# A fused H3 and MLP kernel on one core: all four convolution blocks through the factored transform, in smaller matmul tiles

## The chip, the cores and the metric

The kernel runs on one core of a Trainium2 chip. Its time is the device time of one execution in microseconds (us). Two runs of the kernel before took 268.71 and 269.87 us, a median of 269.29 us. The profile below is of one more execution.

## The reference

Two layers, each an H3 mixer (A) and a channel MLP (B), run over a sequence of 2048 tokens with 512 channels. Both layers use the same weights, and k and v are inputs, so the long convolution of `kv` is the same in both layers and is computed once.

```python
def _A_ref(q, k, v, shift_k, ssm_k, ssm_D):          # S = 2048, D = 512
    k_shift = sum over t of k_pad[:, t:t + S, :] * shift_k[:, ks - 1 - t]   # 4 taps
    kv = k_shift * v
    y = irfft(rfft(kv padded to 2S) * rfft(ssm_k padded to 2S))[:S]         # causal, per channel
    y = y + kv * ssm_D
    return q * y
def _B_ref(x, w1, b1, w2, b2):                       # F = 1376
    h = gelu(layernorm(x) @ w1 + b1)
    return h @ w2 + b2
x = A_q
x = x + _A_ref(layernorm(x), A_k, A_v, A_shift_k, A_ssm_k, A_ssm_D)
x = x + _B_ref(layernorm(x), B_w1, B_b1, B_w2, B_b2)
# and both once more
```

## The kernel before, in words

**Blocks.** The sequence is cut into four blocks of 512 tokens, numbered 0 to 3. The causal convolution is done block by block in a frequency domain of 512 odd frequencies: K0 to K3 are the transforms of the four pieces of the filter, U0 to U3 those of the four blocks of kv, and output block j is the inverse transform of the sum of U(a) times K(j-a) for a from 0 to j. Everything is bf16 in one large SBUF arena, with each buffer's place given in the table PLACE.

**Pieces and their order.** The program is a list of named pieces. The string ORDER gives the order in which they are issued and, behind the point, the engine: P (TensorE, PE), D (VectorE, DVE), A (ScalarE, ACT), G (GpSimd, POOL), S (the SP queue, for DMAs). Each engine works through its pieces strictly in that order. A digit behind P is the PSUM slot: four slots, p0 to p3, of two banks each. The names are, with the block first among the digits:

- lK, lk, lv, lx, w1, w2: loads of filter, k, v, q and the weights; lT, lF, lW, lM, lY: loads of the transform tables
- KT, kt: PE transposes of the filter and of k (L373, L394); kv: the 4-tap shift as matmuls with diagonal matrices (L414), and kvm: the product with v on DVE (L425)
- KD, UD: a direct transform of a block (L451), 8 matmuls of 128x128x512 for each quarter of the frequencies
- KS, US: first stage of the factored transform (L476), 128x128 tiles; Kx, Ux: two DMAs each that regroup its result from partition to partition (`regroup`, L294); KW, UW: second stage (L485) in 64x64 tiles
- ks: swaps of real and imaginary halves of K between partitions, by DMA (L436)
- T: products U times K on DVE (L507); V: first inverse stage (L520), 64x64 tiles; Vx: its regroup by DMA; Y: second inverse stage (L533)
- a letter e behind a PE piece's name is its evacuation from PSUM, 128x1024 each, on ACT (L248) or DVE (L250)
- sa, pa, aa, ga, sb, pb, ab: LayerNorms and the gate x + q*y of layer l and block g (the index is 2g+l); dw and dr: the normed activations go out to DRAM and come back transposed; m1, ge, m2, re: the MLP (L621 in six pieces of up to two 128-column groups, GELU on ACT L628, L641, residual L649); st: output stores

**Which block goes which way.** `DK = {0, 1}` and `DU = {0, 1}` send blocks 0 and 1 of K and U through the direct transform (L446 to L467), with 1 MB of tables tabT. Blocks 2 and 3 go through the factored one. The filter's partner K1 adds K0's swapped halves on DVE (L457).

**What sets the order around the change.** The first MLP matmul, piece m101 on L621, needs the convolution of block 0, its gate and two LayerNorms. Before it PE has the transforms; behind it PE alternates between MLP pieces and the transforms that are left.

## Time and profile before

| | us |
|---|---|
| median of two runs | 269.29 (268.71 and 269.87) |
| profiled execution, span from first to last instruction | 269.2 |
| PE busy in it | 246.4 |
| ACT busy, DVE busy | 144.9, 178.0 |
| first matmul starts | 4.59 |
| first MLP matmul (m101) starts | 87.35 |
| last matmul ends | 262.66 |

The profiled execution's own time is its span, 269.2 us, which lies between the two timed runs. PE's busy time counts a matmul until its result is out, so pipelined matmuls overlap, and a busy PE is not PE at its peak. A time such as "379 ns mean" is the latency of one matmul, and the pace of a run of them is its length divided by their number. PEclk is the granted TensorE clock. "Idle before" a group is time in which that engine stood still, with what ended it.

### The profile page before, as it was taken

What the parts mean: (1) busy time and instruction counts of PE and PEld (TensorE: products, weight loads), DVE (VectorE), ACT (ScalarE), POOL (GpSimd) and SP (SyncE); (2) the same over time, 40 slices, a digit from 0 to 9 for tenths busy, and PEclk for the clock granted to TensorE, in tenths of its full rate; (3) what the DMA queues carried; (4) which work ended last, traced back from release to release, by engine and by line L of the source; (5) the groups of instructions that cost most, each with busy time, mean ns of one, the idle gap of its engine ahead of it and who ended that gap; (6) DMA issues with size and microseconds to landing.
All of it is one profiled execution on the core that took longest, in us unless ns stands there. A gap on an engine that the chain in (4) does not pass through costs nothing.

```text
span 269.2 us, 4359 instructions
## 1 busy us (share of the span) xinstructions
PE 246.4 (92%) x1664; PEld 116.2 (43%) x1664; DVE 178.0 (66%) x293; ACT 144.9 (54%) x187; POOL 45.6 (17%) x89
## 2 busy tenths in 40 slices
PE   3699975999939999999999999999999999999990
PEld 3354533544324444544444444444444444444440
DVE  1558792599846997997999996598770088405021
ACT  2248915579826776698676577600489008303600
POOL 3125300001500003212062015320311011200000
PEclk9999997799977999999999999999999999999997
DMA  6996993496666791767566004135502300330045
GB/s 195 316 220 171 236 289 77 121 243 162 201 177 160 203 305 54 171 147 212 138 162 150 0 2 116 44 100 133 121 0 78 78 2 0 117 78 2 0 108 127
DMA packets 37927, 35.11 MB, mean 130 GB/s; under 512 B 17777, under 2 KB 33650, under 8 KB 37650
## 3 DMA queue, kind: packets, MB, share of 16 engines
q1 hardware_dynamic: 37442, 33.68, 47.7%
q0 software_dynamic: 464, 1.15, 1.5%
q8 instruction: 13, 0.21, 0.4%
q14 instruction: 8, 0.07, 0.1%
HBM read 12.80 MB, written 5.77 MB: 69 GB/s over the span
## 4 chain that ended last, share of the span: by engine, by line
PE 80%; DMA 8%; ACT 4%; DVE 2%; issue 1%; SPq 1%; POOL 1%; ACTq 0%; DVEq 0%; POOLq 0%
PE p L641 28%; PE p L621 28%; PE p L520 7%; PE p L451 6%; PE p L476 3%; ACT arena L248 3%; DMA arena<-tabT 3%; PE p L414 3%; DMA arena<-arena 3%; DMA arena<-in_B_w_dram 3%; PE p L533 2%; PE p L485 1%; SPq L316 1%; ACT arena L287 1%; DVE arena L425 1%
## 5 line engine op out<-in xcount | busy, mean ns | idle before, releaser
L248 ACT ACTIVATE arena<-p 128x1024 bf16<-128x1024 f32 (+2 forms) x66 | 67.8, 1075 | 43.5 <-PE p L451 10.3
L628 ACT ACTIVATE arena<-p,B 128x512 bf16<-128x512 f32 (+1 forms) x88 | 54.7, 687 | 57.1 <-PE p L621 56.3
L621 PE MATMUL p<-arena 128*128 128x512 bf16 (+1 forms) x352 | 78.0, 379 | 0.0
L641 PE MATMUL p<-arena 128*128 128x512 bf16 (+1 forms) x352 | 77.6, 379 | 0.0
L621 PEld LDWEIGHTS <-arena 128*128 128x128 bf16 (+1 forms) x352 | 34.8, 100 | 41.4 <-issue 1.7
L641 PEld LDWEIGHTS <-arena 128*128 128x128 bf16 (+1 forms) x352 | 33.9, 98 | 42.0 <-issue 1.5
L277 POOL TENSOR_TENSOR lrs<-lrs,mhalf 128x2 f32<-128x2 f32 (+1 forms) x29 | 25.7, 888 | 152.0 <-DVE lrs L271 94.7
L507 DVE TENSOR_TENSOR arena<-arena 128x2048 bf16<-128x2048 bf16 (+1 forms) x36 | 46.6, 1336 | 3.1 <-ACT arena L248 1.3
L649 DVE TENSOR_TENSOR arena<-p,arena 128x1024 bf16<-128x1024 f32 (+1 forms) x18 | 19.5, 1102 | 43.2 <-PE p L641 34.8
L267 DVE BATCH_NORM_STATS2 lst<-arena 128x6 f32<-128x512 bf16 x64 | 40.7, 682 | 0.3
L451 PE MATMUL p<-arena 128*128 128x512 bf16 x128 | 32.0, 406 | 2.6 <-DMA arena<-tabT 2.3
L287 ACT ACTIVATE arena<-arena,lnm,lrs 128x512 bf16<-128x512 bf16 x30 | 22.6, 811 | 7.9 <-POOL lnm L282 7.7
L520 PE MATMUL p<-arena,Mt 64*64 64x512 bf16 x320 | 22.2, 416 | 0.0
L451 PEld LDWEIGHTS <-arena 128*128 128x128 bf16 x128 | 12.9, 104 | 19.7 <-issue 5.1
L425 DVE TENSOR_TENSOR arena<-p,arena 128x1024 bf16<-128x1024 f32 x8 | 9.7, 1222 | 10.3 <-PE p L414 7.3
L289 DVE TENSOR_SCALAR arena<-arena,lmv,lrs 128x512 bf16<-128x512 bf16 x34 | 13.1, 433 | 4.7 <-POOL lrs L277 2.6
L520 PEld LDWEIGHTS <-Mt 64*64 64x64 bf16 x320 | 9.0, 114 | 9.6 <-issue 3.5
L593 DVE TENSOR_TENSOR arena<-arena 128x2048 bf16<-128x2048 bf16 (+1 forms) x9 | 9.9, 1105 | 4.0 <-ACT arena L248 3.7
L373 PE MATMUL p<-IDt,arena 128*128 128x128 bf16 x64 | 5.1, 242 | 8.2 <-DMA arena<-in_A_ssm_k_dram 4.6
L250 DVE COPY arena<-p 128x1024 bf16<-128x1024 bf16 (+1 forms) x6 | 5.2, 866 | 11.0 <-PE p L373 5.7
L476 PE MATMUL p<-arena,Ft 128*128 128x512 bf16 x48 | 12.0, 380 | 0.0
L250 DVE CAST arena<-p 128x1024 bf16<-128x1024 f32 x8 | 9.8, 1220 | 3.1 <-PE p L451 1.6
(44 smaller groups left out, 108.3 us busy)
## 6 DMA issues: line engine op xcount, KB each, us to landing
arena<-arena SPq DMA_DIRECT2D x80, 128.0 KB, 2.4
lnd<-arena SPq DMA_DIRECT2D x14, 256.0 KB, 2.2
arena<-in_A_ssm_k_dram SPq DMA_DIRECT2D x4, 512.0 KB, 8.5
arena<-in_A_k_dram SPq DMA_DIRECT2D x4, 512.0 KB, 4.5
arena<-arena SPq DMA_DIRECT2D x8, 256.0 KB, 3.7
arena<-in_A_v_dram SPq DMA_DIRECT2D x3, 512.0 KB, 8.6
arena<-in_A_q_dram SPq DMA_DIRECT2D x6, 256.0 KB, 8.8
out_dram<-arena SPq DMA_DIRECT2D x12, 128.0 KB, 2.4
```

What stands on the lines that cost most here:

```text
L248: nc.scalar.activation(dst, src, AF.Copy)
L267: nc.vector.bn_stats(lst[:, i, :], xg[:, i, :])
L277: nc.gpsimd.tensor_tensor(self.rs[:, a:b], self.rs[:, a:b], mhalf[:, a:b], ALU.pow)
L287: nc.scalar.activation(dst[:, i, :], xg[:, i, :], AF.Identity, bias=self.nm[:, i:i + 1], scale=self.rs[:, i:i + 1])
L451: nc.tensor.matmul(o[:, r, :], at(f"TD{i}", (n * 2 + r) * P, [[1, P]]), at(src, n * D, [[1, D]]), start=n == 0, stop=n == 3)
L476: nc.tensor.matmul(o[:, R, :], Ft[:, f, R, :], at(t, n * D, [[1, D]]), start=s == 0, stop=s == len(terms) - 1, skip_group_check=True)
L507: e.tensor_tensor(at(t, 0, [[2 * D * w, 2], [1, 2 * D * w]]), at(f"U{a}", 2 * i * D, [[0, 2], [1, 2 * D * w]]), at(f"K{kk}", 2 * i * D, [[ ...
L520: nc.tensor.matmul(o[64 * r:64 * r + 64, e, :], Mt[64 * e:64 * e + 64, 2 * i + r, s, :], at(f"T{j}{a}{i // TW[j]}", (s * 2 * TW[j] + 2 * ( ...
L621: nc.tensor.matmul(o[0:m, x, :], at("W1", ct * F + ft * P, [[1, m]]), at(LT, ct * 4 * P, [[1, 4 * P]]), start=ct == 0, stop=ct == CT - 1)
L628: nc.scalar.activation(at(HT, ft * 4 * P, [[1, 4 * P]], 0, m), o[0:m, x, :], AF.Gelu_apprx_tanh, bias=B1[0:m, ft:ft + 1])
L641: nc.tensor.matmul(o[:, x, :], at(HT, ft * 4 * P + t * P, [[1, P]], 0, m), at("W2", ft * D, [[1, D]], 0, m), start=ft == 0 and i not in RE ...
L649: nc.vector.tensor_tensor(xs, psum(pe, [2, D])[:, 0:len(tt), :], xs, ALU.add)
```

## The change

The direct transform, its tables tabT, the swaps by DMA (`ks`) and the sum on K1 (`both`) are gone. All four blocks of K and U go through the factored transform, and real and imaginary part lie side by side in the free dimension. The tiles change: the first stage has two 64x128 tiles (rows by columns of the array) at a time in place of one 128x128, the second stage eight 64x32 tiles in place of four 64x64, and V eight 32x64 tiles in place of four 64x64. V now covers half of a block's frequencies in one piece, with four banks of PSUM and two evacuations (Ve, Vf). PSUM is one tile of eight banks, and the digit behind P is now the first bank. The filter's transposes come as two halves of 64 columns, k's shifted copies need one more copy on DVE (kd), k and v are loaded with two DMAs each instead of one. ORDER and PLACE are new throughout. The MLP's arithmetic is the same.

```diff
-DK = {0, 1}
-DU = {0, 1}
...
-    F = np.zeros((128, 2, 2, 128))
-    W = np.zeros((128, 8, 64))
-    M = np.zeros((128, 8, 2, 64))
-    T = np.zeros((4, 128, 4, 2, 128))
+    F = np.zeros((128, 2, 128))
+    W = np.zeros((128, 8, 2, 32))
+    M = np.zeros((128, 2, 2, 3, 64))
...
-        pf = [ps.tile([P, 1024], F32, name=f"p{i}") for i in range(NPS)]
+        pall = ps.tile([P, 8, 512], F32, name="pall")
...
-                            nc.tensor.transpose(o[:, n, cc, :], at(f"Kraw{j}", cc * L + c * nn + n, [[4, P]]), IDt[:])
+                            for R in range(2):
+                                nc.tensor.transpose(o[64 * R:64 * R + 64, n, cc, :], at(f"Kraw{j}", cc * L + 4 * R + c * nn + n, [[8, 64]]), IDt[:])
...
+            def twice(it, j=j):
+                e = nc.vector if it["eng"] == "D" else nc.gpsimd
+                e.tensor_copy(at(f"kT{j}", 1, [[KI, CT * 4], [1, 63]]), at(f"kT{j}", 128, [[KI, CT * 4], [1, 63]]))
...
-        def swaps(j):
...
-                        for p in range(2):
-                            queue(it["eng"]).dma_start(at(f"K{j}", 8 * D + c * w, [[1, w]], 64 * e + 32 * p, 32), at(f"K{j}", c * w, [[1, w]], 64 * e + 32 - 32 * p, 32))
...
-                if j in (DK if X == "K" else DU):
-                    for i in range(4):
-                        def mms(o, i=i, src=src):
-                            for r in range(2):
-                                for n in range(4):
-                                    nc.tensor.matmul(o[:, r, :], at(f"TD{i}", (n * 2 + r) * P, [[1, P]]), at(src, n * D, [[1, D]]), start=n == 0, stop=n == 3)
...
                 for n in range(4):
                     def mms(o, n=n, terms=terms):
                         for s, (t, f) in enumerate(terms):
                             for R in range(2):
-                                nc.tensor.matmul(o[:, R, :], Ft[:, f, R, :], at(t, n * D, [[1, D]]), start=s == 0, stop=s == len(terms) - 1,
-                                                 skip_group_check=True)
+                                nc.tensor.matmul(o[:, R, :], Ft[64 * R:64 * R + 64, f, :], at(t, n * D, [[1, D]], 64 * R, 64), start=s == 0, stop=s == len(terms) - 1)
...
-                        for e in range(2):
-                            for r in range(2):
-                                nc.tensor.matmul(o[64 * e:64 * e + 64, r, :], Wt[64 * r:64 * r + 64, 2 * i + e, :],
-                                                 at(f"zi{X}{j}", (2 * i + e) * D, [[1, D]], 64 * r, 64), start=True, stop=True, skip_group_check=True)
+                            for q in range(4):
+                                for kk in range(2):
+                                    nc.tensor.matmul(o[32 * q:32 * q + 32, kk, :], Wt[64 * kk:64 * kk + 64, 4 * g + q, p, :],
+                                                     at(f"zi{X}{j}", (4 * g + q) * D, [[1, D]], 64 * kk, 64), start=True, stop=True)
...
-                                    nc.tensor.matmul(o[64 * r:64 * r + 64, e, :], Mt[64 * e:64 * e + 64, 2 * i + r, s, :],
-                                                     at(f"T{j}{a}{i // TW[j]}", (s * 2 * TW[j] + 2 * (i % TW[j]) + r) * D, [[1, D]], 64 * e, 64),
-                                                     start=2 * a + s == 0, stop=2 * a + s == n - 1, skip_group_check=True)
+                        for t in range(4):
+                            for kk in range(2):
+                                for q in range(4):
+                                    nc.tensor.matmul(o[64 * kk:64 * kk + 64, q, :], Mt[32 * q:32 * q + 32, g, kk, (0, 2, 2, 1)[t], :],
+                                                     at(f"T{j}{a}{g}", (2 * t + kk) * D, [[1, D]], 32 * q, 32), start=a == 0 and t == 0, stop=a == j and t == 3)
...
 ORDER = """
...
-ge74.A m170.P0 ge72.A m173.P3 ge70.A m175.P2 ge73.A ge75.A m271.P1 m272.P0 re71.D st71.S st32.S m273.P3 re72.D st72.S
...
+US03e.A Ux03.S US00e.A sa20.D pa20.G Ux00.S Kx02.S KT10.P0 ke1.G Kx00.S sa02.D sa00.D lv2.G aa20.D KT10e.A KS11.P0
...
+ge55.A m154.P6 ge54.A ge50.A m153.P6 ge53.A m252.P6 m250.P2 re60.D st30.S st32.S st10.S sa70.D re62.D sa72.D pa70.G
...
+ge71.A m172.P0 ge72.A m170.P4 ge70.A m174.P0 ge74.A m175.P4 ge75.A m272.P4 re72.D st72.S m270.P5 m273.P4 m271.P0 re52.D
...
```

**Place 1, PE, the first transposes of a further filter block.** Before, this is KT20 (L373), which reads the loaded filter and writes slot p3; the last matmul above it is of a direct transform, KD11 (L451). DMAHW names are the SP queue's DMA semaphores, of which there are eight that the queue's DMAs take in turn.

```order
L451 MATMUL p_135<-arena 128x512
L373 LDWEIGHTS arena [waits DMAHW7_49,DMAHW6_49,DMAHW4_49]
L373 MATMUL p_138<-IDt,arena 128x128 [waits Activation_49]
L373 LDWEIGHTS arena
L373 MATMUL p_138<-IDt,arena 128x128
```

After, it is KT10 (L333), behind the first stage of U0 (US02, US03, US01, US00 on L402).

```order
L402 LDWEIGHTS Ft
L402 MATMUL pall<-arena,Ft 128x512
L333 LDWEIGHTS arena [waits DMAHW4_49,DMAHW5_49,DMAHW3_49,DMAHW6_49,DMAHW2_49,DMAHW7_49,DMAHW1_49,DMAHW0_49]
L333 MATMUL pall<-IDt,arena 64x128 [waits Activation_49]
L333 LDWEIGHTS arena
```

The transposes now wait for DMAs on all eight semaphores instead of three, and the matmuls right above them are the four pieces whose results these DMAs carry.

**Place 2, SP queue, the DMAs around the first blocks.** Before, behind the load of K1's piece of the filter, the swaps of K0 (L436) stand between table and block loads.

```order
L316 DMA arena<-in_A_ssm_k_dram 128x4x512 [waits DMAHW6_49]
L436 DMA arena<-arena 32x2048 [waits DMAHW7_49,Activation_49]
L436 DMA arena<-arena 32x2048 [waits DMAHW0_49]
L316 DMA Mt<-tabM 128x1024 [waits DMAHW1_49]
L436 DMA arena<-arena 32x2048 [waits DMAHW2_49]
L436 DMA arena<-arena 32x2048 [waits DMAHW3_49]
L316 DMA Yt<-tabY 128x64 [waits DMAHW4_49]
```

After, behind the same load, come the regroups of K0 and U0, two DMAs to a piece: Kx03, Kx01, the table lW, then Ux02, Ux01, Ux03, Ux00 and Kx02.

```order
L276 DMA arena<-in_A_ssm_k_dram 128x4x512 [waits DMAHW2_49]
L276 DMA arena<-arena 16x8x512 [waits DMAHW3_49,Activation_49]
L276 DMA arena<-arena 16x8x512 [waits DMAHW4_49]
L276 DMA arena<-arena 16x8x512 [waits DMAHW5_49,Activation_49]
L276 DMA arena<-arena 16x8x512 [waits DMAHW6_49]
L276 DMA Wt<-tabW 128x512 [waits DMAHW7_49]
L276 DMA arena<-arena 16x8x512 [waits DMAHW0_49,Activation_49]
L276 DMA arena<-arena 16x8x512 [waits DMAHW1_49]
L276 DMA arena<-arena 16x8x512 [waits DMAHW2_49,DVE_49]
```

The swaps are gone, and ten regroup DMAs stand in one row between US02's evacuation and KT10.

**Place 3, PE, the end of the last MLP block.** Before, the last m1 piece (m175, the last 96 hidden columns, L621) writes slot p2 (printed p_137), and the m2 piece behind it (m271, L641) writes slot p1 (p_136).

```order
L621 LDWEIGHTS arena
L621 MATMUL p_137<-arena 96x512
L641 LDWEIGHTS arena [waits Activation_49]
L641 MATMUL p_136<-arena 128x512
L641 LDWEIGHTS arena [waits Activation_49]
```

After, m175 (L543) and m272 (L561) both stand on bank 4 in ORDER.

```order
L543 LDWEIGHTS arena
L543 MATMUL pall<-arena 96x512
L561 LDWEIGHTS arena
L561 MATMUL pall<-arena 128x512 [waits Activation_49]
L561 LDWEIGHTS arena
```

The first m2 matmul, which writes PSUM, now has a wait for ACT of its own: the GELU that reads the bank of the piece just ahead of it.

462 lines of the change are left out of this document (195 added, 267 removed).

## The prediction

> **What bounds the kernel now.** I read the page's busy line and chain first, then a table of four stretches cut at the first matmul (4.59), at the first MLP matmul m101 (87.35) and at the last result of PE (262.66).
>
> ```profile
> PE 246.4 (92%) x1664; PEld 116.2 (43%) x1664; DVE 178.0 (66%) x293; ACT 144.9 (54%) x187; POOL 45.6 (17%) x89
> PE 80%; DMA 8%; ACT 4%; DVE 2%; issue 1%; SPq 1%; POOL 1%; ACTq 0%; DVEq 0%; POOLq 0%
> ```
> ```profile
> core 0: us, PE busy (x) PEld busy (x) DVE busy (x) ACT busy (x) POOL busy (x), PEclk, DMA share, GB/s
> 0.00:4.59 4.59, 0.00 (x0) 0.00 (x0) 0.00 (x0) 1.28 (x1) 2.55 (x11) 1.00 0.57 193
> 4.59:87.35 82.76, 71.14 (x612) 36.73 (x613) 57.39 (x84) 48.96 (x50) 14.07 (x28) 0.92 0.75 198
> 87.35:262.66 175.31, 175.30 (x1056) 79.46 (x1052) 119.96 (x209) 94.67 (x137) 28.93 (x50) 1.00 0.37 97
> 262.66:269.20 6.54, 0.00 (x0) 0.00 (x0) 0.69 (x1) 0.00 (x0) 0.00 (x0) 0.71 0.52 122
> ```
>
> From 87.35 on PE stands still for 0.01 us: there, less PE work is less time, and each new wait of PE is lost time. Ahead of it PE is idle for 82.76 − 71.14 = 11.6 us, while ACT and DVE are busy for 49 and 57 of the 83 us. So the time is 4.59 to the first matmul + 246.4 busy + 11.7 idle + 6.54 tail = 269.2. The span stands between the two timed runs, so I forecast against 269.2.
>
> **PE's work.** The groups that the change replaces, and two runs for the pace:
>
> ```profile
> L451 PE MATMUL p<-arena 128*128 128x512 bf16 x128 | 32.0, 406 | 2.6 <-DMA arena<-tabT 2.3 <-ACT arena L248 0.4
> L476 PE MATMUL p<-arena,Ft 128*128 128x512 bf16 x48 | 12.0, 380 | 0.0
> L485 PE MATMUL p<-arena,Wt 64*64 64x512 bf16 x64 | 6.2, 412 | 4.9 <-DMA arena<-arena 4.9
> L520 PE MATMUL p<-arena,Mt 64*64 64x512 bf16 x320 | 22.2, 416 | 0.0
> L520 PEld LDWEIGHTS <-Mt 64*64 64x64 bf16 x320 | 9.0, 114 | 9.6 <-issue 3.5 <-DVE arena L507 0.4
> ```
> ```profile
> 90.46 3.56 PE p L621 x16
> 158.47 7.03 PE p L520 x128
> ```
>
> A full-array matmul takes 3.56/16 = 0.22 us. The 64x64 tiles take 7.03/128 = 0.055, so four run side by side in one pass of 0.22. Their 320 weight loads of 0.114 us would fill 36.5 us end to end, but PEld is busy for 9.0: they overlap by four too. Removed: 32.0 + 12.0 + 6.2 + 22.2 = 72.4 us, which is 128 + 48 + 16 + 80 = 272 passes (59.8) and 12.6 for changes of tile shape and slower stretches over 64 pieces, 0.2 a piece. Added: the first stage has 88 matmuls (8 for K0, 16 for each other K, 8 for each U) in pairs, 44 passes; the second 256 in eights, 32 passes; V 640 in eights, 80 passes. That is 156 passes or 34.3 us, and 72 pieces at 0.2 are 14.2. PE: 246.4 − 72.4 + 48.5 = 222.5, so 24 us less, **if eight small tiles run side by side**, which no row here shows. If only four do, V takes 35.1 instead of 17.6 and the second stage 14.1 instead of 7.0.
>
> The Trainium skill, "TensorE: Matmul & The Clock Gate", section LDWEIGHTS, gives a weight load as columns/1.2 ns, estimated 53 ns for V's 64 columns. One after another, eight would be 0.43 us and V 34 us, as with four tiles. The PEld row above has loads of 64 columns overlapping by four, so it doesn't hold as a serial cost here, and the sum goes without it.
>
> **PE's waits.** PE has less to do, but what feeds it stays: evacuations, regroups, and their order. First from PE's timeline and from the chain of waits (start, length, what):
>
> ```profile
> 4.59 1.89 PE L373 MATMUL p<-IDt,arena 128*128 128x128 bf16 x16 [4.59 <-DMA arena<-in_A_ssm_k_dram]
> 6.28 1.91 PE L394 MATMUL p<-IDt,arena 128*128 128x128 bf16 x16
> 10.45 6.47 PE L451 MATMUL p<-arena 128*128 128x512 bf16 x16 [2.25 <-DMA arena<-tabT]
> 16.85 1.95 PE L414 MATMUL p<-arena 64*128 64x256 bf16 x56
> 42.56 1.06 PE L373 MATMUL p<-IDt,arena 128*128 128x128 bf16 x16 [3.60 <-DMA arena<-arena]
> ```
> ```profile
> 19.15 1.21 DVE arena L425
> 33.30 0.56 PE p L520 x8
> 47.14 1.82 PE p L414 x27
> 57.54 0.99 PE p L414 x28
> ```
>
> Then the regroups' time to landing (DMA issues of the page), ten of their issues on SP's timeline, and the groups of ACT, DVE and PE by shape:
>
> ```profile
> arena<-arena SPq DMA_DIRECT2D x80, 128.0 KB, 2.4
> ```
> ```profile
> 61.10 6.42 SPq L316 DMA_DIRECT2D arena<-arena  x10
> ```
> ```profile
> L248 ACT ACTIVATE arena<-p 128x1024 bf16<-128x1024 f32 x60 | 58.7, 1024 | 33.8 <-PE p L451 10.3 <-PE p L520 9.9 <-PE p L485 7.2
> L248 ACT ACTIVATE arena<-p 128x2048 bf16<-128x2048 bf16 x4 | 7.4, 1873 | 5.2 <-DMA arena<-arena 5.2
> L628 ACT ACTIVATE arena<-p,B 128x512 bf16<-128x512 f32 x80 | 49.9, 687 | 40.2 <-PE p L621 39.4 <-DMA arena<-arena 0.8
> L287 ACT ACTIVATE arena<-arena,lnm,lrs 128x512 bf16<-128x512 bf16 x30 | 22.6, 811 | 7.9 <-POOL lnm L282 7.7
> L556 ACT ACT_TABLE_LOAD x1 | 1.3, 1283 | 0.0
> L250 DVE CAST arena<-p 128x1024 bf16<-128x1024 f32 x8 | 9.8, 1220 | 3.1 <-PE p L451 1.6 <-PE p L533 1.4 <-PE p L476 0.2
> L250 DVE COPY arena<-p 128x1024 bf16<-128x1024 bf16 x4 | 2.8, 689 | 7.2 <-PE p L373 5.7 <-ACT arena L248 1.4
> L457 DVE SCALAR_TENSOR_TENSOR arena<-arena,sgn,p 128x1024 bf16<-128x1024 bf16 x4 | 5.1, 1278 | 1.4 <-PE p L451 1.4
> L373 PE MATMUL p<-IDt,arena 128*128 128x128 bf16 x64 | 5.1, 242 | 8.2 <-DMA arena<-in_A_ssm_k_dram 4.6 <-DMA arena<-arena 3.6
> L641 PE MATMUL p<-arena 128*128 128x512 bf16 x320 | 74.3, 379 | 0.0
> ```
>
> A change of tile shape costs 0.12: eight L520 are two passes, 0.44, and took 0.56. (The 0.2 a piece above holds slower stretches too.)
>
> I walk down the new order and take each place where PE has nothing to run.
>
> (a) Up to US02. The 2.25 us for tabT goes. But U0 can't start before v is loaded and both kvm are done; before, these end at 19.15 + 1.21 = 20.4, and with the table wait gone I take 17.5. PE has some 8.5 us to do in the 12.9 us since 4.59 (KT0 1.9, kt0 1.9, kt10 1.9, both kv 1.95, KS0 0.9): **4.5 idle** (2.3 to 6).
>
> (b) KT10 (place 1). It waits on all eight DMA semaphores, that is for Ux01, Ux03, Ux00 and Kx02. Before, such transposes, KT20, waited 3.60 us for regroups, with direct transforms ahead to fill the time. Now: US02 and its evacuation 1.4, ten DMAs issued at 0.64 each (nine to the last: 5.8), landing 2.4: 9.6 us from US02, of which US02 to US00 fill 0.9. **8.7 idle** (3.6 to 9). Behind KT10 on PE stands everything else.
>
> (c) KS11 needs KT10's evacuation, 128x2048 on ACT, 1.87, and the hand-overs: **2.2 idle**.
>
> (d) KS11 to US12: ACT has 20 evacuations in a row, 1.024 and a gap each, 21 us; DVE has some 19 beside it: eight products, kvm twice and four evacuations at 1.22, kd1 and a LayerNorm. PE's work is 8.8 us of passes and kv (four KS1 1.76, three US1 0.66, twelve second-stage pieces 2.64, V0 1.76, kv10 and kv11 1.98) and 2.3 of tile changes, so **10 idle** (6 to 12). Before, a direct piece of 1.76 us on PE stood against each evacuation of 1.02.
>
> The Trainium skill, "TensorEngine Tiling (Array Packing)", section PSUM Bottleneck, speaks against this change: it says that tiling speeds up TensorE but not the evacuation, so that the PSUM copy may become the bottleneck. The rows agree in kind: a second-stage piece is 0.22 us on PE against 1.02 on ACT.
>
> (e) KT20 again stands behind regroups: V0's eight and Ux10, Ux11, Ux13, six, 9.0 us of issue, some 2.5 of it covered: **6.5 idle** (3.6 as KT20 before, to 9).
>
> (f) From there to m101: ACT has kt20's 1.87, 15 evacuations (15.8), two LayerNorm rows (1.6) and the GELU table (1.3), 20.6 us, and Y1 waits for V1's regroup, 2; PE's work is 13.6 (KS2 1.76, UW1 0.88, Y0 and Y10 1.3, V1 3.5, kv2 2.0, KT20 and LT 1.9, US20 0.2, and 17 changes of shape 2.0): **9 idle** (5 to 11).
>
> (g) Place 3. Seven times PE writes the bank whose GELU has just become possible: m145 to m242, m135 to m232, m165 to m260, m155 to m154 to m153 to m252, m175 to m272. Each costs the result's latency (0.16: 379 ns less the pace of 220), the GELU 0.687 and two semaphores, about 0.95: **6.7** (4 to 7.5). Nothing else is left to hide it, since PE takes its pieces in order.
>
> Idle in sum: 4.5 + 8.7 + 2.2 + 10 + 6.5 + 9 + 6.7 = 47.6, where 11.7 stood.
>
> Edits at nothing: the swaps' 24 issues leave SP, but 32 regroups join it, priced in (b) and (e). The four K1 sums on DVE (1.28 each) go and four copies kd come, which no row shows: 0.69 as the L250 copy of that size or 1.22 as the cast, taken at 0.7; DVE has that to spare in (d). KT's transposes in halves are twice as many and, in pairs, take the 5.1 us of L373; if halves don't pair, 5 more, most of it in the front's gaps. k and v cost four more issues each; w1, w2 and lv move to POOL, where a root of a LayerNorm waits at most one or two issues. The tail of 6.54 (residual, store) stays.
>
> **Sum:** 4.6 + 222.5 + 47.6 + 6.5 = 281.2, so **281 us**, 4.4% slower. m101 would start near 85 us: hardly earlier than the 87.35 now, with more of blocks 2 and 3 still to do behind it.
>
> **Rivals.** The time is 233.6 + the idle, so break-even is 35.6 us of idle.
>
> *PE stays the bound (faster).* The waits in (b), (d), (e) and (f) come from reading an order; if DVE and ACT share the evacuations well and the regroups land while other pieces run, the idle is that of before, 11.7, and the time 245; with half of my terms, 257. It decides for faster below 30 us of idle. For it: ACT and DVE have slack in the front, 49 and 57 of 83 us. Against: PE's 3.60 us at KT20 shows that such a transpose does wait for regroups, and now there are more of them and fewer fillers. 0.14.
>
> *The terms are half as large in the front (no change).* Idle of 30 to 41, 264 to 275: SP's issues start earlier, (e) is covered by (d). 0.19.
>
> *Eight tiles don't overlap (much slower).* V's second half (blocks 2 and 3, seven tenths) stands where PE is the bound: +12, the rest partly in gaps, together +14: 295. For it: only four have been seen. Against: their weight loads overlap without loss. 0.12.
>
> *That the change isn't what it says:* the order has no swaps and no L451 left, so no chance of its own.
>
> The clock is in the range, not a rival:
>
> ```profile
> 40.00:50.00 10.00, 6.92 (x90) 4.40 (x92) 3.64 (x4) 4.67 (x3) 0.26 (x1) 0.68 0.40 97
> ```
>
> After the 3.60 us gap a kv piece took 1.82 instead of 0.99, at a granted clock of 0.68 in that stretch. Three longer gaps stand in the new front; the 0.2 a piece holds such stretches in part, and they cost up to 5 more.
>
> **Numbers.** My forecast (273 to 291) has 0.55. It reaches down into no change and up into the fourth case; the range that leaves out the faster case and the top is 264 to 296. About 2% (263.9 to 274.6) is what a measurement can tell from no change: faster 0.14, same 0.19, slower 0.67.
>
> **What would show it.** Right: PE busy near 222; KT10 (L333) idle for 5 to 9 us on a DMA arena<-arena; L402 and L413 rows behind ACT L206; L561 with idle before it on ACT L550, about 0.9 a time; m101 at 82 to 88. Wrong: V (L441) well above 25 us busy means that the tiles don't overlap; PE idle under 30 us in all means that the front was covered and the kernel is faster.

## The result, and the profile after

The changed kernel takes 295.41 us (295.20 and 295.62) against 269.29 us: 1.093 times as long, with an interval of 1.074 to 1.111. Run again on another chip with four runs, beside the kernel before, it took 295.87 against 268.09 us, 1.103 (1.096 to 1.110). The medians here and below leave out every run that took over 1.5% longer than the fastest of its kernel on its chip, among them one of e5_loads (316.18) and one of e12_all (483.30), so that e12_all has 282.14 us and not the 282.80 that the expectations behind it go by. The forecast was 281: the direction holds, the loss is twice as large.

First the page of the kernel after, its busy line and its chain by engine:

```profile
PE 235.5 (80%) x2133; PEld 112.5 (38%) x2152; DVE 177.3 (60%) x300; ACT 163.0 (56%) x204; POOL 50.0 (17%) x93
PE 65%; DMA 14%; ACT 6%; SPq 5%; issue 5%; DVE 1%; POOL 1%; ACTq 0%; DVEq 0%; POOLq 0%
```

PE is busy for 10.9 us less than before, and DMA's share of the chain goes from 8% to 14%. This page lacks 19 of the 2152 matmuls; the page of the second run (c_after below) has them all, with PE busy for 237.3 us and 11% for DMA. The table of four stretches, cut as before at the first matmul, at the first MLP matmul m101 and at PE's last result (PE busy, PEld, DVE, ACT, POOL, then the granted clock, the DMA engines' share and GB/s):

```profile
0.00:4.51 4.51, 0.00 (x0) 0.00 (x0) 0.00 (x0) 1.28 (x1) 3.52 (x13) 1.00 0.51 146
4.51:98.31 93.80, 52.19 (x722) 29.24 (x722) 50.37 (x78) 49.83 (x52) 13.80 (x27) 0.72 0.78 183
98.31:288.89 190.58, 183.29 (x1413) 83.23 (x1430) 126.24 (x222) 111.90 (x151) 32.63 (x54) 0.99 0.34 82
288.89:293.50 4.61, 0.00 (x0) 0.00 (x0) 0.69 (x1) 0.00 (x0) 0.00 (x0) 0.78 0.43 101
```

The front, up to m101, has grown from 82.8 to 93.8 us, though PE has 19 us less to do in it. PE is idle there for 41.6 us. Behind m101, 15.3 us have been added: the pieces of blocks 2 and 3 that had stood in the front, and 7.3 us of idle time (6.2 in c_after).

Then PE's timeline, the rows with the long waits (the bracket is the idle time ahead of the row and what ended it) and two rows on the pace:

```profile
21.94 1.04 PE L402 MATMUL pall<-arena,Ft 64*128 64x512 bf16 x8 [2.06 <-DVE arena L386]
31.77 2.18 PE L333 MATMUL pall<-IDt,arena 128*64 128x128 bf16 x32 [8.79 <-DMA arena<-arena]
35.91 3.37 PE L402 MATMUL pall<-arena,Ft 64*128 64x512 bf16 x16 [1.96 <-ACT arena L206]
50.47 1.06 PE L413 MATMUL pall<-arena,Wt 64*32 64x512 bf16 x16 [4.33 <-issue]
71.56 2.18 PE L333 MATMUL pall<-IDt,arena 128*64 128x128 bf16 x32 [7.05 <-DMA arena<-arena]
96.28 0.62 PE L455 MATMUL pall<-arena,Yt 128*64 128x512 bf16 x4 [3.41 <-DMA arena<-arena]
...
195.00 7.11 PE L441 MATMUL pall<-arena,Mt 32*64 32x512 bf16 x256
279.22 9.67 PE L561 MATMUL pall<-arena 128*128 128x512 bf16 x43 [0.77 <-ACT arena L550]
```

The waits stand where the walk through the order had put them: US02 at 21.94, KT10 with 8.79 us, KS11 with 1.96, KW110 (50.47), KT20 with 7.05, Y10 (96.28). KW110's row names no releaser; in c_after it is a regroup (DMA arena<-arena), and in the chain below a regroup lands at 49.47, just ahead of it. The tiles do what was forecast: 256 V matmuls in 7.11 us are 32 passes of 0.22, eight tiles side by side. And here is the part of the chain of waits that the forecast did not have (start, length, what):

```profile
6.13 13.28 DMA arena<-in_A_v_dram
...
42.52 6.95 DMA arena<-arena
...
90.01 5.46 DMA arena<-arena
```

Regroups on the chain take 6.95 and 5.46 us to land. The forecast used the page's median for all of them, 2.4 us, and 2.7 is the median in the page of the kernel after.

### The profile page after: what moved, and what is told of

Same layout as the page of the kernel before. It is cut to its first block, busy times and chain, and to the rows that moved or that the text cites. A ratio compares the mean times of both kernels' runs of the same rounds, so it can differ in the third digit from the quotient of the medians.

```text
span 293.5 us, 5396 instructions
## 1 busy us (share of the span) xinstructions
PE 235.5 (80%) x2133; PEld 112.5 (38%) x2152; DVE 177.3 (60%) x300; ACT 163.0 (56%) x204; POOL 50.0 (17%) x93
## 4 chain that ended last, share of the span: by engine, by line
PE 65%; DMA 14%; ACT 6%; SPq 5%; issue 5%; DVE 1%; POOL 1%; ACTq 0%; DVEq 0%; POOLq 0%
PE pall L561 26%; PE pall L543 23%; DMA arena<-arena 9%; PE pall L441 8%; SPq L276 5%; DMA arena<-in_A_v_dram 5%; ACT arena L206 3%; ACT arena L550 2%; PE pall L413 2%; PE pall L333 2%; PE pall L402 2%; PE pall L455 1%; POOL arena L276 1%; DVE arena L386 1%; ACT arena L245 1%
## 5 line engine op out<-in xcount | busy, mean ns | idle before, releaser
L206 ACT ACTIVATE arena<-pall 128x1024 bf16<-128x1024 f32 (+2 forms) x85 | 85.5, 1072 | 71.8 <-PE pall L455 19.9
L550 ACT ACTIVATE arena<-pall,B 128x512 bf16<-128x512 f32 (+1 forms) x88 | 56.8, 692 | 43.4 <-PE pall L543 43.1
L561 PE MATMUL pall<-arena 128*128 128x512 bf16 (+1 forms) x340 | 77.5, 379 | 3.7 <-ACT arena L550 3.1
L543 PE MATMUL pall<-arena 128*128 128x512 bf16 (+1 forms) x345 | 79.3, 382 | 1.5 <-ACT arena L550 0.8
L561 PEld LDWEIGHTS <-arena 128*128 128x128 bf16 (+1 forms) x352 | 33.8, 98 | 46.6 <-issue 7.4
L543 PEld LDWEIGHTS <-arena 128*128 128x128 bf16 (+1 forms) x352 | 34.5, 101 | 44.2 <-issue 6.7
L431 DVE TENSOR_TENSOR arena<-arena 128x2048 bf16<-128x2048 bf16 x40 | 47.3, 1219 | 5.8 <-ACT arena L206 5.6
L566 DVE TENSOR_TENSOR arena<-pall,arena 128x1024 bf16<-128x1024 f32 (+1 forms) x18 | 19.7, 1104 | 50.3 <-PE pall L561 50.3
L441 PE MATMUL pall<-arena,Mt 32*64 32x512 bf16 x640 | 23.2, 439 | 2.8 <-ACT arena L206 2.8
L333 PE MATMUL pall<-IDt,arena 128*64 128x128 bf16 x128 | 8.7, 317 | 20.4 <-DMA arena<-arena 15.8
L208 DVE CAST arena<-pall 128x1024 bf16<-128x1024 f32 x9 | 11.0, 1224 | 22.4 <-PE pall L413 9.5
L402 PE MATMUL pall<-arena,Ft 64*128 64x512 bf16 x88 | 17.1, 470 | 5.9 <-ACT arena L206 3.1
L413 PE MATMUL pall<-arena,Wt 64*32 64x512 bf16 x256 | 12.3, 438 | 8.6 <-issue 4.3
L441 PEld LDWEIGHTS <-Mt 32*64 32x64 bf16 x640 | 12.3, 120 | 13.1 <-issue 8.4
L333 PEld LDWEIGHTS <-arena 128*64 128x64 bf16 x128 | 8.0, 215 | 21.5 <-DMA arena<-arena 16.6
L516 DVE TENSOR_TENSOR arena<-arena 128x2048 bf16<-128x2048 bf16 (+1 forms) x9 | 9.9, 1103 | 3.9 <-ACT arena L206 3.7
```

The lines of the kernel that those rows point to most:

```text
L206: nc.scalar.activation(dst, src, AF.Copy)
L333: nc.tensor.transpose(o[64 * R:64 * R + 64, n, cc, :], at(f"Kraw{j}", cc * L + 4 * R + c * nn + n, [[8, 64]]), IDt[:])
L402: nc.tensor.matmul(o[:, R, :], Ft[64 * R:64 * R + 64, f, :], at(t, n * D, [[1, D]], 64 * R, 64), start=s == 0, stop=s == len(terms) - 1)
L431: e.tensor_tensor(at(t, p * 4 * D, [[2 * D, 2], [1, 2 * D]]), at(f"U{a}", (p * 2 + g) * 2 * D, [[0, 2], [1, 2 * D]]), at(f"K{kk}", g * 2 * ...
L441: nc.tensor.matmul(o[64 * kk:64 * kk + 64, q, :], Mt[32 * q:32 * q + 32, g, kk, (0, 2, 2, 1)[t], :], at(f"T{j}{a}{g}", (2 * t + kk) * D, [ ...
L543: nc.tensor.matmul(o[0:m, x, :], at("W1", ct * F + ft * P, [[1, m]]), at(LT, ct * 4 * P, [[1, 4 * P]]), start=ct == 0, stop=ct == CT - 1)
```

## The experiments

All runs are compared with the control, which is the changed kernel on the chip of three of the other runs. The kernel before took 266.6 to 268.1 us on the five chips that were used, so the table also has each run's time less that of the kernel before on its own chip (above before). Start times also vary from run to run: e3_banks leaves the front as it was, and its m101 starts at 100.10, 2.3 us behind the control's.

| run | edit | time, us | above before | m101 starts |
|---|---|---|---|---|
| e1_warm | idle matmuls in the waits | 295.81 | 29.2 | 97.62 |
| e2_kt10 | KT10 ahead of U0's regroups | 297.44 | 30.9 | 99.75 |
| e3_banks | other PSUM banks | 290.52 | 23.9 | 100.10 |
| e4_vfirst | v0 loaded ahead of k1 | 300.57 | 32.8 | 103.08 |
| e5_loads | six loads later | 295.84 | 28.1 | 95.75 |
| e6_three | e3, e4 and e5 | 292.10 | 24.4 | 99.11 |
| c_after | control | 295.87 | 27.8 | 97.76 |
| e7_queue | v1 to v3 on the SP queue | 295.13 | 27.0 | 93.10 |
| e10_x1 | x1 later, on the SP queue | 298.36 | 30.3 | 102.08 |
| e8_comb | e3, e5, e7 and e10 | 288.34 | 20.2 | 94.94 |
| e11_w2 | w2 later, on the SP queue | 295.44 | 28.2 | 97.66 |
| e12_all | e3, e5, e7 and e11 | 282.14 | 14.9 | 89.24 (e12_look) |
| e13_allkt | the same and e2 | 277.85 | 10.6 | 87.10 |
| e12_look | e12_all once more, for its trace | 281.87 (one) | 14.2 | 89.24 |
| e14_best | e13's front in a new order | 282.12 | 14.5 | 83.98 |
| e15_start | v0 ahead of k1, kt10 behind KT10 | 295.00 | 27.3 | 99.40 |
| e16_start13 | the same edit on e13_allkt | 277.15 | 9.5 | 84.54 |

**The clock.** The sum of the forecast lacked 13 us, and PE's busy time had 13 us more than forecast. In the front the granted clock is 0.72, so the first theory was that PE's own pieces had become slow.

> The changed kernel with 132 idle matmuls on PE that compute nothing that is used, put into the seven long waits of the front (24 of 128 columns ahead of kt01; of 512 columns: 36 ahead of KT10, 8 ahead of KS11, 4 ahead of KW001, 16 ahead of KW110, 30 ahead of KT20, 14 ahead of Y10). Theory A, the clock: PE's own work in the front ran at the granted clock of 0.50 from 25 to 40 us and from 50 to 86 us, and that is the 13 us that my sum lacked; with the clock held up, the front's own pieces go at full pace, the first MLP matmul moves from 98.3 to 87-90 us and the time from 295.4 to 283-287. Rival B, the waits: ACT's evacuations, the regroups and their order pace the front and PE's pace is absorbed in them; first MLP matmul at 95 or later, time 291 or more.

```diff
-... Kx02.S KT10.P0 ...
+... Kx02.S wm1.P0 KT10.P0 ...
+        def warm(n, rhs):
...
+            return lambda it: [nc.tensor.matmul(psum(it, [512])[:, 0:w], IDt[:], r, start=True, stop=True) for _ in range(n)]
```

Each warm piece is n matmuls of constants whose results nobody reads; seven of them stand in ORDER, of which wm1 is shown. The front of this run in one stretch, and the two groups of idle matmuls in it (L575):

```profile
4.44:97.62 93.18, 72.99 (x854) 40.11 (x855) 49.84 (x78) 49.58 (x52) 13.67 (x27) 0.87 0.80 182
```
```profile
L575 PE MATMUL pall<-Wt,IDt 128*128 128x512 bf16 x108 | 25.9, 397 | 1.1 <-DMA Wt<-tabW 1.1
L575 PE MATMUL pall<-IDt 128*128 128x128 bf16 x24 | 1.9, 252 | 0.0
```

The granted clock rose from 0.72 to 0.87, and the front's own pieces took 72.99 − 25.9 − 1.9 = 45.2 us of PE instead of 52.2. m101 came at 97.62, against 98.31 and 97.76 without, and the time did not move. Seven microseconds of PE less, and no gain: the slow clock only stretches pieces inside waits that last anyway. Theory A falls.

**KT10's wait.**

> KT10, the first transposes of the second filter block, stands ahead of the regroups of U0 in the program (PE's and SP's own rows keep their order), so that it no longer waits for their DMAs. Theory A (the wait of 8.8 us at KT10 is a cost of its own, term b): most of it goes, less what the second stage of block 0 then waits for the same regroups; 5 to 7 us less, 288-291. Rival B (the regroups are needed two pieces later anyway): the wait comes back ahead of KW001 (L413) and the time is 293-296.

```diff
-US02.P0 US02e.A Ux02.S US03.P2 US01.P6 US01e.D Ux01.S US00.P4 US03e.A Ux03.S US00e.A sa20.D pa20.G Ux00.S Kx02.S KT10.P0
+US02.P0 US02e.A US03.P2 US01.P6 US01e.D US00.P4 KT10.P0 Ux02.S Ux01.S US03e.A Ux03.S US00e.A sa20.D pa20.G Ux00.S Kx02.S
```

PE's timeline of this run:

```profile
23.36 2.18 PE L333 MATMUL pall<-IDt,arena 128*64 128x128 bf16 x32 [0.62 <-DMA arena<-arena]
27.51 3.60 PE L402 MATMUL pall<-arena,Ft 64*128 64x512 bf16 x16 [1.97 <-ACT arena L206]
35.68 0.62 PE L413 MATMUL pall<-arena,Wt 64*32 64x512 bf16 x8 [4.58 <-DMA arena<-arena]
40.96 1.91 PE L413 MATMUL pall<-arena,Wt 64*32 64x512 bf16 x32 [4.65 <-DMA arena<-arena]
```

KT10 runs 8.4 us earlier, at 23.36, and its wait is down to 0.62. But the second stage behind it waits twice for regroups, 4.58 and 4.65, and KW001 starts at 40.96, where it had started at 40.75. The time, 297.44, shows no gain. The rival was right for this edit alone: the wait at KT10 had hidden a later one of the same end.

**PSUM banks.**

> Other PSUM banks for twelve MLP pieces of the last three blocks, so that no m2 piece writes the bank of the piece just ahead of it (m232, m165, m150 to m155, m250, m252, m270 to m273). Theory (term g): the five waits of 0.71 to 0.83 us on a GELU in the trace go, 3.9 us in sum, 291.5. Rival (the wait is for the GELU's result as m2's input, not for the bank): nothing goes, 295.

```diff
-m135.P0 ge35.A m232.P0 ... m165.P4 ge65.A m260.P4 ... m155.P6 ge55.A m154.P6 ge54.A ge50.A m153.P6 ge53.A m252.P6 ... m175.P4 ge75.A m272.P4
+m135.P0 ge35.A m232.P4 ... m165.P6 ge65.A m260.P4 ... m155.P2 ge55.A m154.P6 ge54.A m153.P4 ge53.A m252.P2 ... m175.P4 ge75.A m272.P5
```

290.52 us, 5.35 below the control, or 3.9 by what each is above the kernel before on its own chip. From m101 to PE's last result it takes 185.6 us where the control takes 191.5, though m101 itself came later here. No wait on L550 of over 0.2 us is left. The term was of the right kind and size.

**Loads in the front: one at a time.** With the clock out and KT10's wait moving on, what was left was the transfers. The DMA engines are busy for 78% of the front.

> The changed kernel with the two loads of v0 ahead of those of k1 on the SP queue; nothing else. In the changed kernel v0 lands at 19.4 us and U0's first stage, which waits for it, starts at 21.9, 4 us later than my walk had it. Theory C (the front is paced by transfers that share the DMA engines with loads): U0's first stage starts 2 to 4 us earlier and KT10, KS11 and the regroups behind it with it; part of it is lost again in the regroups that are slow around 42 to 50 us, so 1 to 3 us less, 292-294. Rival A (clock, PE) and rival B (evacuations): under 1 us.

```diff
-lk0.S kt01.P0 ls.S lk1.S KS00.P2 ... kt10e.D lv0.S
+lk0.S kt01.P0 ls.S lv0.S lk1.S KS00.P2 ... kt10e.D
```

U0's first stage came later, not earlier. In PE's timeline of this run k1's transposes, which stand ahead of kv0 in PE's order, now wait for k1 for 5.10 us:

```profile
18.78 1.86 PE L354 MATMUL pall<-IDt,arena 128*128 128x128 bf16 x16 [5.10 <-DMA arena<-in_A_k_dram]
25.51 1.04 PE L402 MATMUL pall<-arena,Ft 64*128 64x512 bf16 x8 [1.32 <-DVE arena L386]
```

The edit exchanged one wait for another in PE's queue, and the run says nothing on what v0 alone would be worth; that it is slower by 4.7 us does show that a delay at the start reaches the end in full.

> The changed kernel with six loads moved to later places, as they are not needed ahead of the first MLP matmul: K3, k3, x2, x3 and v3 behind it, v2 some 25 us later; 3 MB, of which 2.5 MB leave the front. Theory C: the regroups that took 6.95 us ahead of KW110 and 5.46 us ahead of Y10 land in 2.4 to 3.5, as the page has for the median; 4 to 8 us less, 287-291, with the wait of 4.3 us ahead of KW110 gone. Rival B (evacuations on ACT set the pace there): the waits move to ACT and the time falls by under 2 us.

```diff
-sa00.D lv2.G ... KW000e.D lx2.S KW010.P0 KW010e.A lv1.G ... lK3.S ... lx3.S ... lv3.G ... lk3.S
+sa00.D ... KW000e.D KW010.P0 KW010e.A lv1.G ... w4.G lv2.G ... Ux20.S lK3.S ... Ux22.S lk3.S lx2.S ... on2.G lv3.G ... Ux21.S lx3.S
```

Y10's wait went from 3.41 (4.85 in the control) to 1.17 us and m101 came at 95.75; but KW110's wait, which should have gone, rose to 6.35, and the time did not fall. For v2 the edit missed its aim. It was to go some 25 us later, and POOL's timeline of this run has it 8 us later, right behind v1 (40.52) and ahead of w2 (45.47), at the very time of K1's regroups:

```profile
42.37 1.03 POOL L276 DMA_DIRECT2D arena<-in_A_v_dram  x2
```

> Both of these and the PSUM banks of the earlier run (worth some 4 us) in one kernel. Theory C: the gains add, 10 to 14 us less, 281-285, still above the kernel before. Rival: the front's gains overlap, as one wait takes the place of another, and only 5 to 8 us are left of the sum, 287-290.

292.10, 3.8 below the control: the banks' gain and nothing more. The rival was nearer. But the run holds e4_vfirst, which alone costs 4.7 us, and its U0's first stage starts at 25.68, so it does not tell what the later loads are worth.

> The changed kernel itself, unaltered, as the control on the chip of the three runs beside it, since the earlier runs were on other chips than the first result: all theories expect 294 to 297 us, first MLP matmul at 98 to 100.

As expected, 295.87, with m101 at 97.76.

> The changed kernel with the loads of v1, v2 and v3 issued on the SP queue instead of POOL's, those of v1 ahead of x2; the same bytes at about the same times. Theory C2 (it is not the bytes: POOL's loads go out in packets of 4 KB beside the regroups' packets of 1 KB, and each regroup packet waits behind one of them, so that a regroup takes 5 to 9 us instead of 2.4 while a POOL load runs; in one queue the regroups that were issued first also finish first): the second stage of K1 (KW110) starts at 46 to 48 instead of 50.5, the wait ahead of Y10 falls under 2 us, time 3 to 6 us below the control. Rival C1 (the sum of bytes is the limit): within 1.5 us of the control. Rival B (evacuations): within 1.5 us too, with ACT as the releaser ahead of KW110.

```diff
-sa00.D lv2.G ... lx2.S KW010.P0 KW010e.A lv1.G ... lv3.G
+sa00.D lv2.S ... lv1.S lx2.S KW010.P0 KW010e.A ... lv3.S
```

Two rows of PE's timeline of this run, ahead of Y10 and behind m101:

```profile
91.67 0.62 PE L455 MATMUL pall<-arena,Yt 128*64 128x512 bf16 x4 [0.48 <-DVE arena L208]
104.63 0.41 PE L413 MATMUL pall<-arena,Wt 64*32 64x512 bf16 x8 [3.60 <-DMA arena<-arena]
```

The same bytes in the other queue: Y10's wait is 0.48 instead of the control's 4.85, and m101 comes at 93.10, 4.7 us earlier. But they did not go at the same times. In SP's order v3 is issued at 93.55, behind Y10, where POOL had issued it at 87.47 in the control; x3 is issued at 89.69 there and at 89.76 here. So it was v3 beside Y10's regroups that made this wait. Whether its queue or only its moment matters this run does not tell, and it does not exclude C1. The time is only 0.7 below the control: v3 now stands ahead of U2's regroups in the SP queue, and KW201 waits 3.60 us for them behind m101. The gain was given back, and KW110 started at 50.21, against 49.35 in the control.

> The changed kernel with the load of x1 (512 KB, on POOL's queue at 2 us, beside the loads of the first filter, k and v blocks) moved to the SP queue behind the regroups of U0, and the statistics that read it behind those of block 0; nothing ahead of 44 us needs it. Theory C: v0 lands 2 to 3 us earlier than 19.4, U0's first stage starts at 19 to 20 instead of 21.9, and all behind it is as much earlier as the later waits let through: 1 to 3 us below the control. Rival (what paces the start is the order on PE, k1's transposes ahead of kv): under 0.7 us.

```diff
-dg.D lx1.G ... US00e.A sa20.D pa20.G Ux00.S Kx02.S KT10.P0 ke1.G Kx00.S sa02.D sa00.D lv2.G
+dg.D ... US00e.A Ux00.S Kx02.S KT10.P0 ke1.G lx1.S Kx00.S sa02.D sa00.D sa20.D pa20.G lv2.G
```

298.36, and U0's first stage at 22.73 against the control's 20.80: no gain at the start. Theory C was wrong on this load.

> All that theory C names, with the banks: v1 to v3 on the SP queue, x1 later, K3, k3, x2, x3 and v3 behind the first MLP matmul, and the PSUM banks. If the front is paced by transfers that stand in each other's way, the first MLP matmul comes at 88 to 92 instead of 98 and the time is 281 to 286, some 10 to 13 below the control. If not, only the banks' 4 us and e5's 1 to 2 remain: 288 to 291.

288.34, 7.5 below the control, m101 at 94.94: on the border of what the rival had. The run holds e10_x1, which alone costs 2.5 us. And something still stood beside K1's regroups. The landing times showed it: in the page of the kernel after, POOL's load of w2 takes longest, and POOL's timeline has its issue at 43.60:

```profile
arena<-in_B_w_dram POOLq DMA_DIRECT2D x1, 1280.0 KB, 15.8
```
```profile
34.25 1.08 POOL L276 DMA_DIRECT2D arena<-in_A_v_dram  x2 [6.02 <-PE pall L333]
39.56 1.01 POOL L276 DMA_DIRECT2D arena<-in_A_v_dram  x2 [4.23 <-PE pall L402]
43.60 1.74 POOL L276 DMA_DIRECT2D arena<-in_B_w_dram  x2
```

The first m2 matmul, which reads w2, starts at 113.28. POOL's pieces have little to wait for, so its loads go out as soon as their space is free, v2 at 34, v1 at 39.6 and w2 at 44, one behind the other, all along K1's regroups (38 to 44) and on to 60 us.

> The changed kernel with the load of w2 (1.28 MB and its last 96 rows) moved from POOL's queue to the SP queue behind the regroups of U1; nothing else. In the changed kernel POOL issues it at 44.25 us, 70 us before its first use, and it lands at 60.0, beside the regroups of K1 and the loads of k2 and K2. Theory C3 (it is this one transfer, which my prediction costed at nothing, that makes the regroups around 42 to 50 us slow): the second half of K1's regroups land in 2.4 to 4 us instead of 5.6 to 7, KW110 starts 2 to 3 us earlier, k2 and K2 land before 58; 2 to 4 us below the control's 295.9. Rival C2 (v1's and v2's loads do it): under 1 us. Rival B (evacuations): under 1 us.

```diff
-V01f.A w4.G ... KS22e.A w3.G w2.G w1.G gd.A
+V01f.A w4.G ... kd2.D Ux12.S w2.S w3.S UW110.P4 ... KS22e.A w1.G gd.A
```

295.44, 0.4 below the control, and KW110 at 49.94: no gain. C3 as one transfer falls: with w2 gone, v1, v2, x2 and k2 are there still.

> w2 late, v1 to v3 on the SP queue, K3, k3, x2, x3 and v3 behind the first MLP matmul, and the PSUM banks. Theory C3 with C2: no regroup of the front takes over 4 us, the first MLP matmul comes at 89 to 92, the time is 281 to 285. Rival (what is left of the front is the chain of first stage, regroup, second stage, product and evacuation in their order): first MLP matmul at 93 or later, 286 to 289.

282.14 us, 13.7 below the control: what w2 (0.4), the queue (0.7) and the later loads (0.0) gave one by one is 1.1 in sum, and together with the banks' 5.4 they give 13.7. So the transfers are worth 8.4 us, or 9.0 by what each run is above the kernel before (23.9 in e3_banks, 14.9 here), and none of the three edits shows it alone. Against e8_comb two things differ, w2 is out of the way and x1 is back in its place, so the step from there is not w2's alone. Where the 8.4 us lie is read from a second run of the same kernel.

> The kernel of e12_all once more, for its trace. If the 7.7 us beyond the banks' gain are the transfers ahead of m101, m101 comes 6 to 8 us ahead of the control's 97.76, at 90 to 92. If they lie behind m101, it comes at 95 to 98, and the stretch behind it is shorter than the 185.6 us that the banks alone left.

The stretch from m101 to PE's last result as one row of the table, and Y10 in PE's timeline:

```profile
89.24:275.49 186.25, 182.16 (x1413) 82.96 (x1430) 126.58 (x222) 112.31 (x152) 31.68 (x54) 1.00 0.39 95
```
```profile
87.81 0.62 PE L455 MATMUL pall<-arena,Yt 128*64 128x512 bf16 x4 [1.10 <-DMA arena<-arena]
```

Y10's wait is 1.10 and m101 comes at 89.24, 8.5 us ahead of the control's 97.76, and the stretch behind it is 186.2 us, as with the banks alone (185.6). So all that the four edits give beyond the banks lies ahead of m101. KW110's wait is down to 0.63 us from the control's 4.16.

> The same with KT10 ahead of U0's regroups, as in the run that moved it alone. There its 8.8 us came back as waits for regroups that took 5.5 and 8.6 us beside POOL's loads; with these out of the way, theory C: the gain stays, 3 to 6 us below the run beside it, 277 to 281. Rival (the regroups' issue, ten in a row at 0.64 us behind KT10, is the limit): within 1.5 us of it.

277.85 us, 4.3 below e12_all on the same chip. The edit that gave nothing alone gives 4.3 here. PE's timeline and the table of the front of this run:

```profile
24.85 2.18 PE L333 MATMUL pall<-IDt,arena 128*64 128x128 bf16 x32 [0.20 <-ACT arena L206]
34.06 0.63 PE L413 MATMUL pall<-arena,Wt 64*32 64x512 bf16 x8 [2.20 <-DMA arena<-arena]
36.71 1.91 PE L413 MATMUL pall<-arena,Wt 64*32 64x512 bf16 x32 [2.02 <-DMA arena<-arena]
63.40 2.18 PE L333 MATMUL pall<-IDt,arena 128*64 128x128 bf16 x32 [6.32 <-DMA arena<-arena]
85.67 0.62 PE L455 MATMUL pall<-arena,Yt 128*64 128x512 bf16 x4 [1.12 <-DMA arena<-arena]
```
```profile
4.19:87.10 82.91, 50.93 (x722) 29.31 (x723) 49.92 (x78) 49.90 (x52) 9.04 (x19) 0.77 0.72 183
```

The front is 82.9 us again, as in the kernel before, and PE is busy in it for 50.93 us at a granted clock of 0.77, nearly the 52.19 at 0.72 of the changed kernel: of the 10.9 us by which it is shorter, 9.6 came out of the waits, which confirms the first experiment from the other side.

**The rest, by a new order.** What remains against the kernel before might be an order that can still be mended.

> e13_allkt with its front in a new order: k0 is loaded ahead of K0's transposes, KT10 stands right behind US00, the loads of x0, k3 and x2 later, and some 60 pieces moved by a few places. Theory: what is left in e13_allkt beyond the kernel before are avoidable waits in the front, 3.0 us ahead of U0, 4.2 ahead of KW001 and KW000, 6.3 at KT20, about half of which an order can fill: m101 at 80 to 82 and 270 to 273 us, which is level with the kernel before and not below it. Rival: these waits are the regroups themselves, which no order hides, and the time stays at 276 to 279 us.

```diff
-lK0.S KT00.P0 KT00e.D lD.S ... lF.S KT01e.A lk0.S ... kt10.P0 ... kt10e.D lv0.S ... lx0.G ... US00.P4 KT10.P0
+lK0.S KT00.P0 lk0.S lb.G KT00e.D lD.S ... lF.S ... lv0.S ... KT10.P0 US00.P4 ... kt10.P6 ... kt10e.D KS11e.A lx0.S
```

(KT10 came to stand just ahead of US00.) Two rows of PE's timeline, U0's first stage and KT20:

```profile
17.90 1.47 PE L402 MATMUL pall<-arena,Ft 64*128 64x512 bf16 x6 [3.52 <-DVE arena L386]
57.50 2.18 PE L333 MATMUL pall<-IDt,arena 128*64 128x128 bf16 x32 [2.96 <-DMA arena<-arena]
```

The front did get shorter, 83.98 us against 87.10, with U0's first stage at 17.90 and half of KT20's wait gone. But the time is 282.12, 14.5 above the kernel before on its chip where e13_allkt is 10.6 (the ratios are 1.054 and 1.042): from m101 to PE's last result the trace has 189.2 us for 185.8. Of the 3.4 us, 1.1 are idle time (189.16 less 184.21 us of PE, against 185.79 less 181.96), the rest is PE's busy time, with a granted clock of 0.92 in the 30 us behind m101 against 1.00. The four runs lie between 279.88 and 283.98. Neither theory said that. No order that was tried comes below the kernel before.

**The start.**

> The changed kernel with v0 loaded ahead of k1, as in e4_vfirst, and k1's transposes kt10 behind KT10 in PE's order, so that no piece ahead of U0 reads k1. If the 4.3 us at the start are v0's place in the SP queue, U0's first stage starts at 17.5 to 19, and if they reach the end, the time is 2 to 4 us below the control, 292 to 294 us. Rival, that the front is held by its transfers later on: U0 starts early too, but KW110 starts at 49 to 51 as in the control, and the time is within 1 us of it.

```diff
-lk0.S kt01.P0 ls.S lk1.S ... kt00e.D kt10.P0 ... kv00.P6 kt10e.D lv0.S kvm00.D ... KT10.P0 ke1.G
+lk0.S kt01.P0 ls.S lv0.S lk1.S ... kt00e.D ... kv00.P6 kvm00.D ... KT10.P0 kt10.P6 kt10e.D ke1.G
```

PE's timeline: k0's transposes, kv00, U0's first stage, KT10, KW110:

```profile
10.65 1.01 PE L354 MATMUL pall<-IDt,arena 128*128 128x128 bf16 x8 [4.08 <-DMA arena<-in_A_k_dram]
15.26 1.89 PE L379 MATMUL pall<-arena 64*128 64x256 bf16 x28 [1.12 <-ACT arena L206]
20.53 1.04 PE L402 MATMUL pall<-arena,Ft 64*128 64x512 bf16 x8 [1.32 <-DVE arena L386]
31.89 2.18 PE L333 MATMUL pall<-IDt,arena 128*64 128x128 bf16 x32 [10.32 <-DMA arena<-arena]
50.00 1.06 PE L413 MATMUL pall<-arena,Wt 64*32 64x512 bf16 x16 [2.55 <-issue]
```

Neither v0 nor k1 is waited for now, and U0's first stage still starts at 20.53, against the control's 20.80. What holds it here is k0: its transposes wait for it up to 10.65, in the control up to 9.14, and kv00, kv01 and the product kvm01 follow one behind the other. The time is 295.00, 27.3 above the kernel before on its chip against the control's 27.8: no gain. KW110 starts at 50.00 against 49.35.

> The same edit on e13_allkt, where the loads stand out of the regroups' way and KT10 ahead of U0's regroups. If the edit is worth nothing in the changed kernel only because the crowd takes it back, it gives 2 to 4 us here: m101 at 83 to 85 and 274 to 276 us. If it is v0's landing itself that is not moved by its place, U0's first stage stays at 22 to 23 and the time at 277 to 279 us.

Here U0's first stage starts at 20.32 instead of 23.21, and m101 comes at 84.54 instead of 87.10: 2.6 of the 2.9 us reach it, though m101 varies by 2.3 us from run to run (e3_banks). The medians, 277.15 and 277.85, and the ratios on the two chips, 1.036 (1.027 to 1.044) and 1.042 (1.035 to 1.048), are too close together to show the gain as time.

## Why the prediction was right and wrong

**Right: where PE would wait, and that it would lose.** The walk had 40.9 us of idle time ahead of m101, and 41.6 were measured; (b) 8.7 against 8.79, (c) 2.2 against 1.96, (e) 6.5 against 7.05. One reading behind (b) and (e) was wrong all the same. The 3.60 us of KT20 in the kernel before, read there as a wait for regroups, were one for a swap of K, which the change removes; the chain of waits of that kernel has it right behind the sum on K1 (L457), and SP's issue at 40.31 is one of L436:

```profile
39.01 1.29 DVE arena L457
...
40.31 2.24 DMA arena<-arena
```

The waits came out right by the walk, not by this example. "PE has less to do, but what feeds it stays" is what happened. The rival in which PE stays the bound is out, as is the one in which eight tiles do not overlap, though its 295 is the time that came: L441 took 0.22 us a pass. The filter's transposes in halves did not pair, which the prediction had left open: 32 of them took 2.13 us at 110.66, where 16 whole ones had taken 1.06, and the group (L333) has 8.7 us where 5.1 were taken.

**Right in kind: (g).** 6.7 us were forecast for seven waits. Five came, 3.91 us in sum; m145 to m242 and m154 to m153 had none, since other pieces stand between or the GELU was early. The banks gave 3.9 to 5.4.

**Wrong: the sum's form.** It added PE's busy time at full pace to PE's idle time. The idle time came out right at 48.9 against 47.6 and the busy time wrong, 235.5 against 222.5, and that suggests that the 13 us are PE's. (c_after, whose page is complete, has 47.5 and 237.3.) For the larger part they are not: in e1_warm 7.0 us of them went with the clock held up, and the time did not move, so at half the clock PE was busy in time in which it would have waited. The idle time that agreed was therefore an agreement by chance too; at full pace it would have been some 7 us more in the front. The sum is also one of a span: it is 12.3 us short of the 293.5 of the profiled execution, and that run's time, 295.20, is 1.7 us longer than its span, which the forecast left out.

**Wrong, the step that failed: the price of the transfers.** Counted by when each piece starts, the walk is right in one stretch: from U0's first stage to KT10 it had 9.6 us, 9.83 were measured. It loses 4.3 us at the start (17.6 against 21.94 for U0's first stage), 5.6 between KS11 and kt20 (21.1 against 26.7), 4.2 between KT20 and m101 (22.6 against 26.8). In each of the three a transfer stands on the chain: "I take 17.5" for v0, which landed at 19.4; and regroups that were all taken at 2.4 and took 6.95 and 5.46. In e12_look, with the loads out of the way, the last two stretches take 22.4 and 23.6 us, near to what the walk had. What was missed stands under *Edits at nothing*: "w1, w2 and lv move to POOL, where a root of a LayerNorm waits at most one or two issues." It asked who waits in POOL's queue, and not what the transfers do once they are out. They go out 10 (v1) to 70 us (w2) ahead of their use, beside the regroups that the new front lives on. Taken out of their way, together with the loads of SP's queue that e5_loads moves, they are worth 8.4 to 9.0 us (e12_all), and they also decide whether KT10's wait of 8.8 us is a cost (4.3 in e13_allkt) or only hides the next one (nothing in e2_kt10). In the walk it stood as a cost of its own. By the column "above before", the 27.8 us that the changed kernel loses are 3.9 for the banks, 9.0 for the transfers and 4.3 for KT10's wait behind them; the 10.6 left in e13_allkt are what the change itself costs in the orders that were tried. Each of these is uncertain by some 2 us, as the intervals of the ratios are 0.7 to 0.9% to each side.

**The 4.3 us at the start** are more than v0's place in the queue. In the kernel after v0 lands last, in the control k1, whose transposes stand ahead of kv00; k0 is late in both. With v0 and k1 out of the way k0 holds U0 at 20.5 (e15_start); with k0 loaded first, x0's loads sent off later and the pieces in a new order U0's first stage starts at 17.90 (e14_best), which is near the 17.5 of the forecast. The table of the stretch from 4.5 to 15 us shows the difference, in the kernel before and in the kernel after:

```profile
4.50:15.00 10.50, 8.15 (x43) 4.99 (x44) 6.27 (x16) 1.94 (x2) 2.61 (x6) 1.00 1.02 282
```
```profile
4.50:15.00 10.50, 5.67 (x54) 3.78 (x54) 3.71 (x7) 3.70 (x4) 1.77 (x4) 1.00 1.03 204
```

The DMA engines are full in both, and move 204 GB/s now where they moved 282. The "17.5" was the old time without the table wait, at the old rate. The rate alone does not decide it, though: e14_best moves 206 GB/s in the same stretch and the control 222.

**Open.** Why the same full engines move less there was not taken apart: POOL's queue has 0.99 MB of those 2.14 now and had 0.53 of 2.96, and k and v come in two transfers of 256 KB where they came in one of 512. How a load slows a regroup is not shown either, only that v3 beside Y10's regroups did (e7_queue), and that the three edits together took most of the waits at KW110 and Y10 away (e12_look). The Trainium skill, "DMA: Bandwidth & Descriptors", section "Queues, rings and completion order", says that each DMA engine takes turns between its queues, a packet at a time. No run here shows it: e7_queue, where Y10's wait fell from 4.85 to 0.48 us, changed v3's queue and its time of issue at once. A run in which a load goes out on either queue at the same moment would tell.

## What to carry to other kernels

A transfer that is moved to another queue is priced by what it runs beside, not only by who waits in that queue: find out when it will be issued with nothing to hold it back, and which small transfers on the critical path land in that time. When several transfers crowd a stretch, taking one away can show nothing, because the others are still there or one moves into its place; take all away at once to learn what the crowd costs, and only then test the waits. And busy time at a low granted clock is not a cost until a run at full clock is faster.
